# First eight and last seven dense units on all 128 rows of TensorE, with both weight halves of a unit in one tile

## The chip, the core and the metric

The kernel runs on one core of a Trainium2 chip. The metric is the device time of one execution in microseconds (us); the kernel before takes 827.67 us, the median of 3 runs (827.59 to 827.92). TensorE is called PE here, its weight loads PEld, VectorE DVE, ScalarE ACT, GpSimd POOL; SP issues most DMAs.

## The reference

Input `x` has 2048 tokens of 512 features. It is normalized, and two branches read the result: attention in a window of 256 tokens (32 heads of 16 features), and a SwiGLU block with 1792 hidden features. The block's output is a gate on the attention's output:

```python
xn = _layernorm(x)
qkv = xn @ wqkv                                  # 512 x 1536
scores = q @ k.T * 16 ** -0.5                    # masked: 0 <= i - j < 256
s = (softmax(scores) @ v) @ wo                   # 512 x 512
b = (silu(xn @ w_gate) * (xn @ w_up)) @ w_down   # 512 x 1792, 1792 x 512
return x + s * silu(b)
```

All of it is float32. Dense products are made of three matmuls: each operand is split into a rounded high part and the low part that is left, and high x high, high x low and low x high are added (`PAIRS`).

## The kernel before

**Units.** The tokens come in four chunks of 512. Dense work is cut into units, each with its own weights: `Proj` (q and k of two head groups, tiles named `a`), `GateUp` (one block of 128 hidden features, `g` and `u`), `Values` and `WideValues` (v, `vp`), `Down` (a part of w_down, `d`), `Wo` and `WideWo` (`s`). Most units have 1024 weight columns (24 steps of 512 columns), the wide ones, `WideValues`, `WideWo` and the longer `Down`, 2048. A name such as `d1_3_0` is chunk 1, part 3, item 0.

**Two lanes.** PE's 128 rows are used as two halves of 64 rows that work side by side. Lane 0 (rows 0 to 63) multiplies the first 64 features of each block of 128, lane 1 (rows 64 to 127) the other 64. Both add into the same PSUM bank, so lane 1 starts an item when lane 0 has ended it (`hand_over`, L1818; `LAG` matmuls are added to be sure). Lane 1 is thus always about one item behind lane 0. Score matmuls (`b` at L1465 for the row maxima, `c` at L1593 for the probabilities) have 48 or 49 rows and fill both lanes in pairs. Visits (`pv`, L1641) multiply probabilities with v in 64x32 pieces.

**Weights.** A raw unit of weights comes by DMA (`wr`). ACT rounds it into the high tile (`wh`, L642), POOL subtracts to get the low tile (`wl`, L647), both in halves of 512 columns. Since lane 1 lags, tile j holds the lower 64 rows of unit j and the upper 64 rows of unit j-1, and lane 1 reads tile `n + 1`. There are `NWH = 14` such tiles, so seven pairs of a high and a low half; a half is given back when both lanes have read it (`used`, L675).

**The order.** Everything is written out by a planner in Python that runs when the kernel is built. It keeps a clock for every engine, takes the unit that is due, and puts score pairs and visits at the places that the tables `EARLY`, `VIS` and `MWU` give. What it writes is the fixed order of instructions on each engine; at run time only semaphores hold an engine back.

**The two ends.** At the start `load_first` (L403) brings `x` and the first weights. `Values` for the first chunk begins as soon as the lower 64 rows of its weights are there, with lane 0 alone, and the transposes of the scaled chunk 0 that follow (`xt_turn`, L702) are made in 64x64 pieces, eight per block of 128 features. At the end the last `Wo` (L1119) evens the lanes out: lane 0 takes 22 of lane 1's 256-column matmuls, for which four DMAs (`rest_low`, L1290) copy upper rows of the attention's output to the lower rows.

Of the kernel before, what the change touches and what calls it, by code (L numbers as in the profile page):

```python
# [17 lines left out]
P = 128  # L18
R = 64
# [40 lines left out]
LAG = 7  # L60
# [18 lines left out]
MOVED = 10  # L79
# [4 lines left out]
OUT = 3.4  # L84
# [11 lines left out]
)  # L96
VIS = (
# [8 lines left out]
def tile_window_attention_swiglu_gate(  # L106
# [296 lines left out]
    def load_first():  # L403
# [66 lines left out]
        def split(raw, j, r, t):  # L470
# [5 lines left out]
            def low(a):  # L476
                hi, lo = (w[half(r)] for w in wtile[j, a // 512][:2])
                nc.gpsimd.tensor_tensor(lo, raw[half(r), a : a + 512], f32(hi), op=ALU.subtract)
                if r == 0 and a:
                    timer(free_at["G"] + SURE, raw_give, raw)  # L480

            def ready(t):
                if (j, r) == (1, 0):
                    low1.append(t)
                else:
                    wready[j, 0] = wready[j, 1] = t
# [28 lines left out]
        split(wr[0], 0, 0, (6.6, 6.85))  # L515
        split(wr[1], 1, 1, (9.35, 10.3))
        split(wr[1], 1, 0, (11.9, 11.9))
# [32 lines left out]
    def half(r):  # L550
        return slice(R * r, R * r + R)
# [5 lines left out]
    class Unit:  # L557
# [3 lines left out]
        def w(self, r, s, a, k):  # L561
            t = wtile[self.n + r, a][s]
            return t.rearrange("p (k n) -> p k n", n=self.cols)[half(r), k, :]

        def wat(self, r, a):
            return wready.get((self.n + r, a))
# [34 lines left out]
    def w_fetch(j):  # L601
        lo, up = weighted.get(j), weighted.get(j - 1)
        if lo is None and up is None:
            return
        parts = [(r, u) for r, u in ((0, lo), (1, up)) if u is not None]
        if lo is None:
            parts.append((0, up))
        box = []

        def go(r, u, last):  # L610
            if not box:
                box.append(raw_take(f"wr{j}"))
            if r == 0 and lo is None:
                move(box[0][half(0)], u[half(1)])
            else:
                move(box[0][half(r), : u.shape[1]], u[half(r)])
            if last and j:
                w_fetch(j + 1)

        for n, (r, u) in enumerate(parts):  # L620
            last = n == len(parts) - 1
            dma(now[0], lambda r=r, u=u, last=last: go(r, u, last),
                lambda t, last=last: w_split(j, t, box[0]) if last else None,
                slack=WSL, can=lambda: box or rfree)

    def w_split(j, t, raw):
        w = [weighted[i].shape[1] if i in weighted else 0 for i in (j, j - 1)]
        both = min(w)
        cuts = [(slice(0, P), a, min(a + 512, both)) for a in range(0, both, 512)]
        if max(w) > both:  # L630
            r = 0 if w[0] > both else 1
            cuts += [(half(r), both, max(w))]
        if j not in weighted:
            cuts = [(slice(0, P), a, a + 512) for a in (0, 512)]
        left = [sum(b <= 512 for _, _, b in cuts), sum(b > 512 for _, _, b in cuts), len(cuts)]

        def high(pr, a, b):
            h = a // 512
            if (j, h) not in wtile:
                w_take(j, h)  # L640
                split_next[0] = (j, 1) if h == 0 and max(w) > 512 else (j + 1, 0)
# [15 lines left out]
        def before(margin, n):  # L657
            at = work_at.get(j, total)
            return lambda: now[0] + max(at - work[0], 0.0) * PRESS - margin + 0.3 * n

        spare = now[0] + max(work_at.get(j, total) - work[0], 0.0) - t - 5.0
# [40 lines left out]
    def xt_turn(c, k):  # L702
        left = [2]
        for r in range(2):
            pb, tag = bank(rb_free, f"xp{c}_{k}_{r}")
            src = pb[:, :256].rearrange("p (t n) -> p t n", n=R)
            hi, lo = (
                xn[c % 2][s][:, k, :].rearrange("p (t r n) -> p t r n", r=2, n=R)[:, :, r, :]
                for s in range(2)
            )  # L710

            def go(t, r=r, pb=pb):
                nc.tensor.matmul(  # L713
                    pb[:, R * t : R * t + R], xt[c, t][half(r), k * P : (k + 1) * P],
                    ident[half(r), half(r)], is_transpose=True, start=True, stop=True,
                )

            def done(t, tag=tag):
                rb_free[tag] = t
                left[0] -= 1  # L720
                if left[0] == 0:
                    xready[c, k] = t
                    if k == KC - 1:
                        for i in range(4):
                            give(xt.pop((c, i)))

            def low(src=src, hi=hi, lo=lo):
                nc.vector.tensor_tensor(lo, src, f32(hi), op=ALU.subtract)

            def finished(t, src=src, hi=hi, low=low, done=done):  # L730
                do("S", t, 0.3, lambda: nc.scalar.activation(hi, src, AF.Copy),
                   lambda t: do("V", t, 0.35, low, done, 0.3), 0.3)

            for t in range(4):
                extra[r].append((128, lambda t=t, go=go: go(t), finished if t == 3 else None))
# [211 lines left out]
    class Wide(Unit):  # L947
# [3 lines left out]
        def w(self, r, s, k):  # L951
            return wtile[self.n + r + k // 2, k % 2][s][half(r)]
# [9 lines left out]
        def gate(self, i, r, m):  # L962
            k = m // 3
            return wready.get((self.n + r + k // 2, k % 2))
# [8 lines left out]
    class Values(Moving):  # L973
# [25 lines left out]
        def gate(self, i, r, m):  # L999
            kp, a, b = (m // 8, 0, m // 4 % 2) if m < 16 else ((m - 16) // 4, 1, 0)  # L1000
            return latest([(lready if a else cready).get((i, kp)), wpart.get((self.n + r, r, b, 512 * kp), 0.0 if self.n + r > 1 else None)])
# [117 lines left out]
    class Wo(Moving):  # L1119
# [15 lines left out]
        def mms(self, i, r, pb):  # L1135
# [3 lines left out]
            todo = [(t, k, PAIRS, None) for t in range(2 - r) for k in range(KC)]  # L1139
            other = [(1, k, p) for k in range(KC) for p in PAIRS]  # L1140
            cut = len(other) if i else MOVED
            todo += [(t, k, [p], xn[1]) for t, k, p in other[:cut]] if r == 0 else [(t, k, [p], None) for t, k, p in other[cut:]]
            for n, (t, k, pairs, moved) in enumerate(todo):
                po = (pb, self.second[i])[t][:, :256]
                tok = slice((2 * i + t) * P, (2 * i + t + 1) * P)
                for a, b in pairs:
                    def go(first, last, n=n, k=k, a=a, b=b, t=t, tok=tok, po=po, moved=moved, pairs=pairs):
                        end = (a, b) == pairs[-1] and [o[0] for o in todo[n + 1 :][:1]] != [t]
                        if moved:
                            act, wt = moved[a][half(0), k, i * P : i * P + P], self.n + 1  # L1150
                        else:
                            act, wt = self.act(k, a)[half(r), tok], self.n + r
                        wt = wtile[wt, k // 2][b].rearrange("p (k n) -> p k n", n=256)[half(r), k % 2, :]
                        mm(po, act, wt, r == 0 and moved is None and (k, a, b) == (0, 0, 0), end)
                        if end and (i, r, t) == (1, 0, 0):
                            hand_over(pos[0], clock[0], 0.0)
                        elif end and i + r:
                            last_part(i, t, po, now[0] + 0.35)
                    yield 256, go, k // 2

        def gate(self, i, r, m):
            if (self.c, self.hf) != (NCH - 1, 1):
                return super().gate(i, r, m)
            if m < 6:
                return 0.0
            if r or m < 6 * KC:
                return self.wat(r, 1)
            return latest([rest.get("t") if rest.get("n") == 4 else None, self.wat(1, 0), self.wat(1, 1)])
# [119 lines left out]
    rest = {}  # L1288

    def rest_low():  # L1290
        for n in range(4):
            def copy(s=n % 2, i=n // 2):
                n = i * 2 * P + P
                move(xn[1][s][half(0), :, i * P : i * P + P], xn[0][s][half(1), :, n : n + P])

            def landed(t):
                rest["n"] = rest.get("n", 0) + 1
# [709 lines left out]
```

## Time and profile before

| what | value |
|---|---|
| median of 3 runs | 827.67 us |
| the profiled execution | 827.96 us |
| its span, first to last instruction | 826.1 us |
| PE busy | 820.2 us (99%), 9874 matmuls |
| POOL / DVE / ACT busy | 640.2 / 503.7 / 497.8 us |
| PE clock granted | 1.00 |
| first dense matmul starts, last one starts | 9.12 us, 822.23 us |

A share of PE counts time in which at least one lane works, so a lane that idles beside the other isn't seen in it. A matmul's own duration is longer than the distance to the next one on its lane, since they are pipelined; what counts is the distance from start to start. One record is about 1.9 us longer than the span because of what lies around the program's first and last instruction.

### The profile page before, as it was taken

How to read it: one execution, taken by the hardware profiler on the slowest of the kernel's cores; microseconds unless marked ns; L12 is line 12 of the kernel's file. 1: busy time of each engine (PE TensorE's matmuls, PEld its weight loads, DVE VectorE, ACT ScalarE, POOL GpSimd, SP SyncE). 2: the span in 40 equal slices, each digit the busy share in tenths (PEclk: the TensorE clock that was granted, in tenths of full speed). 3: DMA queues.
4: the chain of work that ended last, by engine and by line, in shares of the span. 5: the costliest groups of instructions: out<-in, count | busy, mean ns of one | idle time of the engine just before them, and what ended most of it. 6: DMA issues, size and time to landing. Idle time of an engine off the chain costs nothing.

```text
span 826.1 us, 25672 instructions
## 1 busy us (share of the span) xinstructions
PE 820.2 (99%) x9874; PEld 702.4 (85%) x9874; DVE 503.7 (61%) x1545; ACT 497.8 (60%) x949; POOL 640.2 (77%) x898
## 2 busy tenths in 40 slices
PE   8999999999999999999999999999999999999998
PEld 8999888888888888888889888888888888888887
DVE  4246688456657786656648786557546556644235
ACT  6536866465666667456766757546667664566532
POOL 6566878887768799669877789858688976896963
PEclk9999999999999999999999999999999999999999
DMA  6596766686678785577668876566786787864344
GB/s 168 153 214 172 176 155 171 166 192 162 155 198 215 207 226 123 134 204 172 167 151 206 204 197 182 145 168 148 189 189 155 165 175 205 198 134 109 80 124 129
DMA packets 67810, 140.13 MB, mean 170 GB/s; under 512 B 14742, under 2 KB 18326, under 8 KB 67688
## 3 DMA queue, kind: packets, MB, share of 16 engines
q1 hardware_dynamic: 67224, 137.84, 67.7%
q8 instruction: 78, 1.28, 0.7%
q10 hardware_dynamic: 464, 0.66, 0.3%
q14 instruction: 44, 0.36, 0.2%
HBM read 107.74 MB, written 29.62 MB: 166 GB/s over the span
## 4 chain that ended last, share of the span: by engine, by line
PE 99%; DMA 1%; DVE 0%; SPq 0%; issue 0%; DVEq 0%
PE d L693 20%; PE u L693 19%; PE g L693 18%; PE a L693 10%; PE pv L1641 9%; PE c L1593 6%; PE vp L693 6%; PE s L693 6%; PE b L1465 5%; DMA xt<-x 1%; PE xp L525 0%; PE xp L713 0%; DVE st L422 0%; SPq L147 0%; DVE xt L427 0%; PE warm L309 0%
## 5 line engine op out<-in xcount | busy, mean ns | idle before, releaser
L647 POOL TENSOR_TENSOR wl<-wr,wh 128x512 fp32r<-128x512 f32 x238 | 305.8, 1299 | 65.8 <-ACT wh L642 55.2
L1473 DVE CUSTOM_DVE_ANT_0 jk<-b,maskb 128x384 bf16<-128x384 f32 (+2 forms) x512 | 250.2, 528 | 104.8 <-PE b L1465 91.4
L1553 ACT ACTIVATE p<-c 128x512 f32<-128x512 f32 (+2 forms) x384 | 197.9, 569 | 67.0 <-PE c L1593 61.1
L693 PE MATMUL d<-wh,hh 64*128 64x512 f32 x896 | 221.1, 390 | 0.0
L693 PE MATMUL u<-xl,wh 64*128 64x512 f32 x448 | 162.5, 390 | 0.0
L693 PE MATMUL g<-xh,wh 64*128 64x512 f32 x448 | 162.5, 389 | 0.0
L693 PE MATMUL u<-xh,wh 64*128 64x512 f32 x448 | 162.4, 389 | 0.0
L693 PE MATMUL g<-xh,wl 64*128 64x512 f32 x448 | 161.6, 389 | 0.0
L693 PE MATMUL u<-xh,wl 64*128 64x512 f32 x448 | 161.4, 389 | 0.0
L693 PE MATMUL g<-xl,wh 64*128 64x512 f32 x448 | 160.6, 389 | 0.0
L642 ACT ACTIVATE wh<-wr 128x512 fp32r<-128x512 f32 x238 | 144.5, 630 | 24.9 <-PE d L693 17.0
L693 PE MATMUL d<-wl,hh 64*128 64x512 f32 x448 | 158.8, 390 | 0.0
L693 PEld LDWEIGHTS d<-wh,hh 64*128 64x128 f32 x896 | 141.2, 185 | 13.4 <-issue 0.4
L1565 POOL TENSOR_SCALAR_AFFINE_SELECT p<-p 128x256 f32<-128x256 f32 x256 | 101.6, 410 | 40.0 <-ACT p L1553 38.7
L1569 POOL TENSOR_SCALAR_AFFINE_SELECT p<-p 128x256 f32<-128x256 f32 x224 | 91.3, 411 | 9.9 <-ACT p L1553 9.6
L887 POOL TENSOR_TENSOR hh<-h,hh 128x512 fp32r<-128x512 f32 x53 | 68.8, 1298 | 36.4 <-ACT hh L883 34.5
L693 PE MATMUL a<-xh,wh 64*128 64x512 f32 x256 | 96.2, 389 | 0.0
L693 PE MATMUL a<-xl,wh 64*128 64x512 f32 x256 | 95.8, 388 | 0.0
L693 PE MATMUL a<-xh,wl 64*128 64x512 f32 x256 | 95.7, 387 | 0.0
L1465 PE MATMUL b<-k,q 48*128 48x384 f32 (+2 forms) x512 | 90.6, 326 | 0.0
L1593 PE MATMUL c<-q,k 49*128 49x128 f32 (+2 forms) x704 | 89.0, 298 | 0.0
L693 PEld LDWEIGHTS d<-wl,hh 64*128 64x128 f32 x448 | 82.5, 185 | 6.5 <-issue 0.2
(130 smaller groups left out, 1943.2 us busy)
## 6 DMA issues: line engine op xcount, KB each, us to landing
wr<-wgu SPq DMA_DIRECT2D x112, 256.0 KB
wr<-wdn SPq DMA_DIRECT2D x48, 256.0 KB
k<-qkd SPq DMA_DIRECT2D x48, 192.0 KB
wr<-wqk SPq DMA_DIRECT2D x32, 256.0 KB
q<-qkd SPq DMA_DIRECT2D x64, 128.0 KB
od<-ev SPq DMA_DIRECT2D x32, 256.0 KB
qkd<-qkh SPq DMA_DIRECT2D x31, 256.0 KB
qkd<-qkl SPq DMA_DIRECT2D x29, 256.0 KB
```

The costliest lines, as they stand in the source:

```text
L642: nc.scalar.activation(wtile[j, h][0][pr, a - 512 * h : b - 512 * h], raw[pr, a:b], AF.Copy)
L647: nc.gpsimd.tensor_tensor(lo, raw[pr, a:b], f32(hi), op=ALU.subtract)
L693: recent[0] = nc.tensor.matmul(pb, a, b, start=first, stop=last, skip_group_check=True).ins
L887: nc.gpsimd.tensor_tensor(hl[:, 1, :], self.h, f32(hl[:, 0, :]), op=ALU.subtract)
L1465: nc.tensor.matmul(pb[:, :n], qs[u % 3][r : r + 48, p, qb * P : (qb + 1) * P], ks[u % 3][r : r + 48, p, lo : lo + n], start=True, stop=True,)
L1473: nc.vector.tensor_tensor_reduce(junk[:, :n], pb[:, :n], maskb[:, 3 * P - n :], 1.0, -3.0e38, ALU.add, ALU.max, m[:, col : col + 1],)
L1553: nc.scalar.activation(t[:, h, :], pc[:, :n], AF.Exp, scale=DH ** -0.5)
L1565: nc.gpsimd.affine_select(s, s, [[0, 2], [1, P]], ALU.is_ge, 0.0, base=0, channel_multiplier=-1)
L1569: nc.gpsimd.affine_select(s, s, [[0, 2], [-1, P]], ALU.is_gt, 0.0, base=0, channel_multiplier=1)
L1593: nc.tensor.matmul(pc[:, at0 : at0 + w], ks[u % 3][r : r + 49, p, k0 : k0 + P], qs[u % 3][r : r + 49, p, qb * P : qb * P + w], start=(i == ...
L1641: nc.tensor.matmul(pbs[r][0][32 * j : 32 * j + 32, q0:q1], vt[half(r), (4 * c + kb) % VT, VW * (4 * g + j) : VW * (4 * g + j) + 32], t[hal ...
```

## The change

The planner gets a second way to issue dense work. For the first eight units (`NFULL`) and the last seven (`TAIL`) it issues one matmul over all 128 rows where it issued a pair of 64-row matmuls; the units between stay in two lanes. These are 300 matmuls of 512 columns and 192 of 256 columns in the place of as many pairs. Before it changes from one way to the other, the lane that is ahead waits until both have ended the same unit. Both 64-row halves of a unit's weights now lie in one tile (`wtile[self.n]`), so the first DMAs of weights bring 128 rows each. The transposes of chunk 0 are whole 128x128 ones, the evening out at the end with its four DMAs is gone, `LAG` goes from 7 to 3, and the tables that place scores and visits have new numbers. One `WideWo` (chunk 1) comes one unit earlier.

```diff
-LAG = 7
+LAG = 3
-MOVED = 10
+NFULL = 8
+TAIL = 7
+WSH = 0
-OUT = 3.4
+OUT = 3.009
...
-    -0.179, -0.21, -0.095, -0.4, -0.388, 0.119, 0.067, -0.001,
+    -0.106, -0.21, -0.038, -0.4, -0.388, 0.119, 0.067, -0.15,
...
         for a, eng in ((512, nc.scalar), (0, nc.sync)):
-            move(wr[0][half(0), a : a + 512], u0[half(0), a : a + 512], eng)
+            move(wr[0][:, a : a + 512], u0[:, a : a + 512], eng)
         rows(2, nc.scalar)
         rows(3, nc.sync)
         for a in (0, 512):
-            move(wr[1][half(1), a : a + 512], u0[half(1), a : a + 512])
-        move(wr[1][half(0)], u1[half(0)])
+            move(wr[1][:, a : a + 512], u1[:, a : a + 512])
...
         def w(self, r, s, a, k):
-            t = wtile[self.n + r, a][s]
+            t = wtile[self.n, a][s]
...
     def used(r, n, a, t):
-        half_ended.add((r, n, a))
-        j = n + r
-        if all((h, j - h, a) in half_ended or j - h not in weighted or weighted[j - h].shape[1] <= 512 * a for h in range(2)):
-            timer(t, w_end, j, a)
+        for h in range(2) if r == 2 else (r,):
+            half_ended.add((h, n, a))
+        if all((h, n, a) in half_ended for h in range(2)):
+            timer(t, w_end, n, a)
...
+    def both_rows(n):
+        return stream[n][0].n < NFULL or stream[n][0].n >= order[-TAIL].n
+
+    def full():
+        return pos[0] == pos[1] < len(stream) and both_rows(pos[0]) and not any(extra)
...
+    def full_mm():
+        n = pos[0]
+        u, i = stream[n]
...
+        go(m == 0, m == len(todo) - 1)
...
+        pos[:] = [n + 1] * 2
...
         if r == 0:
+            if pos[1] < pos[0] and both_rows(pos[0]):
+                return None
```

Where the first eight units end, PE's order before goes on in two lanes; `wh8_0` is the first high half of tile 8, `g0_4` the first unit behind the eight:

```order
L1465 MATMUL b0_2_0_962<-k0_77,q0_74 128x384
L1465 MATMUL b0_2_1_963<-k0_77,q0_74 128x384
L693 MATMUL g0_4_968<-xh0_81,wh8_0_790 128x512
L693 MATMUL g0_3_877<-xh0_81,wl8_0_791 128x512
L693 MATMUL g0_4_968<-xl0_82,wh8_0_790 128x512
```

At the same place of PE's order now:

```order
L678 MATMUL g0_4_695<-xl0_82,wh8_0_595 128x512
L678 MATMUL g0_4_695<-xh0_81,wl8_0_596 128x512
L678 MATMUL g0_4_695<-xh0_81,wh8_0_595 128x512
L678 MATMUL g0_4_695<-xl0_82,wh8_0_595 128x512
L678 MATMUL g0_4_695<-xh0_81,wl8_0_596 128x512
L678 MATMUL u0_4_738<-xh0_81,wh8_1_603 128x512
```

Before, `g0_4` on lane 0 alternates with `g0_3` on lane 1; now all twelve matmuls of `g0_4` and four of `u0_4` stand on lane 0 before lane 1's first dense matmul, with score pairs among them.

Where chunk 2's `WideValues` (`vp2`) meets chunk 1's last `Down` (`d1_3`), both wide, PE's order before, with `d1_3_0` on lane 0 and `vp2` on lane 1:

```order
L693 MATMUL d1_3_0_7948<-wh63_0_7836,hh1_12_7211 128x512
L693 MATMUL vp2_3_7875<-wh61_0_7486,xh0_81 128x512
L693 MATMUL d1_3_0_7948<-wh63_1_7897,hh1_13_7388 128x512
L693 MATMUL vp2_3_7875<-wl61_0_7487,xh0_81 128x512
L693 MATMUL d1_3_0_7948<-wl63_1_7898,hh1_13_7388 128x512
```

The same units on PE now:

```order
L678 MATMUL d1_3_0_7645<-wh63_0_7489,hh1_12_6910 128x512
L678 MATMUL vp2_3_7576<-wl60_1_7141,xh0_81 128x512
L678 MATMUL vp2_3_7576<-wh60_1_7140,xl0_82 128x512
L678 MATMUL vp2_3_7576<-wh61_0_7196,xh0_81 128x512
L678 MATMUL vp2_3_7576<-wl61_0_7197,xh0_81 128x512
L678 MATMUL vp2_3_7576<-wh61_0_7196,xl0_82 128x512
L678 MATMUL vp2_3_7576<-wh61_1_7274,xh0_81 128x512
L678 MATMUL vp2_3_7576<-wl61_1_7275,xh0_81 128x512
L678 MATMUL vp2_3_7576<-wh61_1_7274,xl0_82 128x512
L678 MATMUL d1_3_0_7645<-wh63_1_7682,hh1_13_7055 128x512
```

Lane 1 now ends `vp2` with seven matmuls that have no partner, and only then comes the half tile `wh63_1`, which lies at the address of `wh60_0` and is written when lane 1 has read that one for the last time; the next eight dense matmuls stand on lane 0 alone.

Where the last seven units begin, PE's order before, in two lanes through `g3_10` and `g3_11`:

```order
L693 MATMUL g3_11_14356<-xh1_83,wh111_0_14089 128x512
L693 MATMUL g3_10_14249<-xl1_84,wh111_0_14089 128x512
L693 MATMUL g3_11_14356<-xl1_84,wh111_0_14089 128x512
L693 MATMUL g3_10_14249<-xh1_83,wl111_0_14090 128x512
L693 MATMUL g3_11_14356<-xh1_83,wl111_0_14090 128x512
```

At the same place now (the last rows of lane 1, then the first ones over 128 rows):

```order
L678 MATMUL u3_10_13975<-xh1_83,wh110_1_13796 128x512
L678 MATMUL u3_10_13975<-xl1_84,wh110_1_13796 128x512
L678 MATMUL u3_10_13975<-xh1_83,wl110_1_13797 128x512
L678 MATMUL g3_11_14064<-xh1_83,wh111_0_13805 128x512
L678 MATMUL g3_11_14064<-xl1_84,wh111_0_13805 128x512
L678 MATMUL g3_11_14064<-xh1_83,wl111_0_13806 128x512
```

Lane 0 has ended `u3_10` when lane 1 still has five matmuls of `g3_10` and all twelve of `u3_10` to do, and `g3_11` doesn't start before they are done.

More of the change, by code (lines that the diff above doesn't have):

```diff
@@ L478, in low @@
                 nc.gpsimd.tensor_tensor(lo, raw[half(r), a : a + 512], f32(hi), op=ALU.subtract)
-                if r == 0 and a:
+                if a:
                     timer(free_at["G"] + SURE, raw_give, raw)
             def ready(t):
-                if (j, r) == (1, 0):
+                if j:
                     low1.append(t)
-                else:
-                    wready[j, 0] = wready[j, 1] = t
+                wready[j, 0] = wready[j, 1] = t
             for a in (0, 512):
@@ L514, in load_first @@
             do("V", lands[i], 1.05 if i != 1 else 1.45, lambda i=i: stats(i), lambda t, i=i: after_stats(t, i), -1.0)
-        split(wr[0], 0, 0, (6.6, 6.85))
-        split(wr[1], 1, 1, (9.35, 10.3))
-        split(wr[1], 1, 0, (11.9, 11.9))
+        split(wr[0], 0, 2, (6.9, 7.9))
+        split(wr[1], 1, 2, (11.0, 11.9))
     def x_turn(i):
@@ L550, in half @@
     def half(r):
-        return slice(R * r, R * r + R)
+        return slice(0, P) if r == 2 else slice(R * r, R * r + R)
     def latest(times):
@@ L561, in w @@
         def w(self, r, s, a, k):
-            t = wtile[self.n + r, a][s]
+            t = wtile[self.n, a][s]
             return t.rearrange("p (k n) -> p k n", n=self.cols)[half(r), k, :]
         def wat(self, r, a):
-            return wready.get((self.n + r, a))
+            return wready.get((self.n, a))
         def inputs(self, i):
@@ L601, in w_fetch, with go @@
     def w_fetch(j):
-        lo, up = weighted.get(j), weighted.get(j - 1)
-        if lo is None and up is None:
+        u = weighted.get(j)
+        if u is None:
             return
-        parts = [(r, u) for r, u in ((0, lo), (1, up)) if u is not None]
-        if lo is None:
-            parts.append((0, up))
         box = []
-        def go(r, u, last):
+        def go(r):
             if not box:
                 box.append(raw_take(f"wr{j}"))
[L613 to L617, printed above, removed]
+            move(box[0][half(r), : u.shape[1]], u[half(r)])
+            if r:
                 w_fetch(j + 1)
[L620 to L623, printed above, removed]
+        for r in range(2):
+            dma(now[0], lambda r=r: go(r), lambda t, r=r: w_split(j, t, box[0]) if r else None,
                 slack=WSL, can=lambda: box or rfree)
     def w_split(j, t, raw):
[L627 to L634, printed above, removed]
+        w = weighted[j].shape[1]
+        cuts = [(slice(0, P), a, a + 512) for a in range(0, w, 512)]
         left = [sum(b <= 512 for _, _, b in cuts), sum(b > 512 for _, _, b in cuts), len(cuts)]
@@ L640, in high @@
                 w_take(j, h)
-                split_next[0] = (j, 1) if h == 0 and max(w) > 512 else (j + 1, 0)
+                split_next[0] = (j, 1) if h == 0 and w > 512 else (j + 1, 0)
             nc.scalar.activation(wtile[j, h][0][pr, a - 512 * h : b - 512 * h], raw[pr, a:b], AF.Copy)
@@ L657, in before @@
         def before(margin, n):
-            at = work_at.get(j, total)
+            at = work_at.get(j + WSH, total)
             return lambda: now[0] + max(at - work[0], 0.0) * PRESS - margin + 0.3 * n
-        spare = now[0] + max(work_at.get(j, total) - work[0], 0.0) - t - 5.0
+        spare = now[0] + max(work_at.get(j + WSH, total) - work[0], 0.0) - t - 5.0
         t += min(max(0.5 * spare, 0.0), 1.5)
@@ L702, in xt_turn, with done, low @@
     def xt_turn(c, k):
[L703 to L709, printed above, removed]
-            )
[L712 to L735, printed above, removed]
+        pb, tag = bank(rb_free, f"xp{c}_{k}")
+        hi, lo = (xn[c % 2][s][:, k, :] for s in range(2))
+        for t in range(4):
+            nc.tensor.matmul(
+                pb[:, P * t : P * t + P], xt[c, t][:, k * P : (k + 1) * P], ident,
+                is_transpose=True, start=True, stop=True,
+            )
+        advance(0.45)
+        def done(t):
+            rb_free[tag] = t
+            xready[c, k] = t
+            if k == KC - 1:
+                for i in range(4):
+                    give(xt.pop((c, i)))
+        def low():
+            nc.vector.tensor_tensor(lo, pb, f32(hi), op=ALU.subtract)
+        do("S", now[0] + 0.2, 0.52, lambda: nc.scalar.activation(hi, pb, AF.Copy),
+           lambda t: do("V", t, 0.61, low, done, 0.3), 0.3)
     def x_wait(c):
@@ L951, in w @@
         def w(self, r, s, k):
-            return wtile[self.n + r + k // 2, k % 2][s][half(r)]
+            return wtile[self.n + k // 2, k % 2][s][half(r)]
         def wneed(self, i, r):
@@ L963, in gate @@
             k = m // 3
-            return wready.get((self.n + r + k // 2, k % 2))
+            return wready.get((self.n + k // 2, k % 2))
         def mms(self, i, r, pb):
@@ L1000, in gate @@
             kp, a, b = (m // 8, 0, m // 4 % 2) if m < 16 else ((m - 16) // 4, 1, 0)
[L1001 removed]
+            return latest([(lready if a else cready).get((i, kp)), wpart.get((self.n, r, b, 512 * kp))])
         def inputs(self, i):
@@ L1138, in mms, with go @@
                 return
[L1139 to L1143, printed above, removed]
+            for t in range(2):
                 po = (pb, self.second[i])[t][:, :256]
                 tok = slice((2 * i + t) * P, (2 * i + t + 1) * P)
[L1146 to L1159, printed above, removed]
+                for k in range(KC):
+                    for a, b in PAIRS:
+                        def go(first, last, k=k, a=a, b=b, t=t, tok=tok, po=po):
+                            end = (k, a, b) == (KC - 1, *PAIRS[-1])
+                            mm(po, self.act(k, a)[:, tok], self.w(r, b, k // 2, k % 2), (k, a, b) == (0, 0, 0), end)
+                            if end:
+                                last_part(i, t, po, now[0] + 0.35)
+                        yield 256, go, k // 2
         def gate(self, i, r, m):
@@ L1163, in gate @@
                 return super().gate(i, r, m)
[L1164 to L1168, printed above, removed]
+            return 0.0 if m % 12 < 6 else self.wat(r, 1)
         def begin(self, i):
@@ L1286, in gates @@
         return all(gready.get((NCH - 1, t), 1e9) <= now[0] for t in ts)
[L1288 to L1297, printed above, removed]
-                rest["t"] = t
-            dma(now[0], copy, landed, 0.0, 128, lambda: NCH - 1 in x_used)
     def x_landed(i):
@@ L1402, in split @@
             oready[c, k] = t
-            if last and all((c, n) in oready for n in range(KC)):
-                timer(t, rest_low)
         def then_r(t):
@@ L1860, in next_mm, with full_ready @@
             u.done(i, banks.pop(n), t, lambda t: fb_free.__setitem__(tag, t))
+    def both_rows(n):
+        return stream[n][0].n < NFULL or stream[n][0].n >= order[-TAIL].n
+    def full():
+        return pos[0] == pos[1] < len(stream) and both_rows(pos[0]) and not any(extra)
+    def full_ready():
+        u, i = stream[pos[0]]
+        if run[0] is not None:
+            return u.gate(i, 2, run[0][1])
+        return latest([bank_time(fb_free), u.inputs(i), u.wneed(i, 2)])
+    def full_mm():
+        n = pos[0]
+        u, i = stream[n]
+        if run[0] is None:
+            banks[n], tags[n] = bank(fb_free, u.name(i))
+            if isinstance(u, Wo):
+                u.begin(i)
+            run[0] = [list(u.mms(i, 2, banks[n])), 0]
+        todo, m = run[0]
+        cols, go, a = todo[m]
+        go(m == 0, m == len(todo) - 1)
+        advance(max(cols * 0.000417, 0.1067) + 0.0025)
+        work[0] += cols * MM / 512
+        if u.last_use(i) and all(o[2] != a for o in todo[m + 1 :]):
+            n2, a = a if isinstance(u, Wide) else (0, a)
+            used(2, u.n + n2, a, clock[0] + 0.2)
+        run[0][1] += 1
+        if run[0][1] < len(todo):
+            return
+        run[0] = None
+        pos[:] = [n + 1] * 2
+        tag = tags.pop(n)
+        u.done(i, banks.pop(n), clock[0] + 0.2, lambda t: fb_free.__setitem__(tag, t))
     def ready(r):
@@ L1911, in tile_window_attention_swiglu_gate @@
             continue
-        times = [ready(0), ready(1)]
+        whole = full()
+        times = [full_ready()] * 2 if whole else [ready(0), ready(1)]
         able = [r for r in range(2) if times[r] is not None and times[r] <= max(clock[r], now[0])]
@@ L1955, in tile_window_attention_swiglu_gate @@
             idle = 0
+            if whole:
+                full_mm()
+                continue
             r = min(able, key=lambda r: clock[r])
```

22 rows, old and new, of tables (EARLY, MWU, VIS) are left out of this document.

## The prediction

> **What bounds the kernel now.** I read the page first, then the chain, PE's waits, the windows by stage, and the timeline of PE at both ends.
>
> ```profile
> PE 820.2 (99%) x9874; PEld 702.4 (85%) x9874; DVE 503.7 (61%) x1545; ACT 497.8 (60%) x949; POOL 640.2 (77%) x898
> PE 99%; DMA 1%; DVE 0%; SPq 0%; issue 0%; DVEq 0%
> PE warm L309 <- DVE warm L304: 1.1, 1, 1.1
> PE xp L525 <- issue: 0.7, 1, 0.7
> PE xp L525 <- DVE xt L427: 0.5, 1, 0.5
> 56.00:770.00 714.00, 714.00 (x8713) 604.38 (x8712) 462.83 (x1466) 447.37 (x856) 570.10 (x828) 1.00 0.71 174
> 822.30:826.10 3.80, 0.20 (x2) 0.00 (x0) 0.93 (x3) 0.00 (x0) 0.75 (x2) 1.00 0.40 138
> ```
>
> PE is the chain (99%). Its waits sum to 2.3 us, all before 9.1 us, and between 56 and 770 us it is busy for 714.00 of 714.00 us. So nothing that another engine does faster can gain there: the time is the sum of the distances between matmuls, plus about 9 us ahead of the first and 3.6 us behind the last. A change gains by shorter distances or by filling a lane that stands empty while the other works, and loses wherever PE is made to wait. The distances, in the timeline of PE:
>
> ```profile
> 788.22 0.39 PE L693 MATMUL g<-xh,wh 64*128 64x512 f32 x1
> 788.45 0.39 PE L693 MATMUL u<-xh,wh 64*128 64x512 f32 x1
> 788.45 0.39 PE L693 MATMUL g<-xl,wh 64*128 64x512 f32 x1
> ...
> 788.90 0.39 PE L693 MATMUL u<-xh,wl 64*128 64x512 f32 x1
> 788.90 0.39 PE L693 MATMUL g<-xh,wh 64*128 64x512 f32 x1
> 821.63 0.28 PE L693 MATMUL s<-wh,xh 64*128 64x256 f32 x1
> ...
> 822.23 0.28 PE L693 MATMUL s<-wh,xl 64*128 64x256 f32 x1
> 6.33 0.27 PE L525 MATMUL xp<-ident,xt 128*128 128x128 f32 x1
> 6.44 0.83 PE L309 MATMUL warm<-warm 128*128 128x128 f32 x6
> ```
>
> Three pairs of 512 columns go from 788.22 to 788.90: 0.227 us a pair. Six lone matmuls of 256 columns start at even distances from 821.63 to 822.23: 0.120 us, the same with or without a partner. Matmuls over all 128 rows exist in one form alone, 128x128 in true f32. They come 0.11 us apart: from 6.33 to 6.44, and (0.83 - 0.275)/5 = 0.111 for the six (0.275 us being one's duration).
>
> **The change part by part.**
>
> *Distances (gain).* No row shows a rounded 128-row matmul of 256 or 512 columns. The nearest is the f32 transpose, about 0.110. From 256 to 512 columns a lane's distance grows by 0.227 - 0.120 = 0.107, which I read as the streaming of 256 columns; the rest is 0.013 in a lane and 0.003 over 128 rows, so a transpose streams as long as 256 columns do, and I take its distance for them. That makes 0.110 and 0.217 for 256 and 512 columns, 0.010 less than a lane each. Over a longer stretch of the chain pairs are a little dearer:
>
> ```profile
> 793.82 14.64 PE d L693 x128
> ```
>
> 64 pairs in 14.64 us are 0.2288 each, by which 512 columns save 0.012. I take 0.011 for 300 + 192 = 492 matmuls: 5.4 us. Bounds: 3.4 us (0.113, what rounding leaves open for the six warm-up matmuls, saves 0.007) and 6.4 us (streaming alone, 0.013).
>
> *Empty lane at the start and the evening out (gain).*
>
> ```profile
> 9.12 0.74 PE L693 MATMUL vp<-wh,xh 64*128 64x256 f32 x4
> 11.43 0.63 PE L693 MATMUL vp<-wl,xh 64*128 64x256 f32 x4
> 11.99 0.66 PE L525 MATMUL xp<-ident,xt 128*128 128x128 f32 x4
> 12.57 0.62 PE L693 MATMUL vp<-wh,xl 64*128 64x256 f32 x3
> 15.06 0.28 PE L693 MATMUL vp<-wl,xh 64*128 64x256 f32 x1
> 15.17 0.28 PE L693 MATMUL vp<-wh,xh 64*128 64x256 f32 x1
> ```
>
> From 9.12 to about 15 one lane works alone. The last `Wo` pays it back by giving 22 of lane 1's matmuls to lane 0, so lane 0 carries 44 more than lane 1: 44 x 0.120 = 5.3 us in which lane 1 is empty, worth half of that, 2.65 us of span. All of it goes.
>
> *Changes of tile shape (gain).* The four matmuls at 11.43 are (0.63 - 0.28)/3 = 0.117 apart, so the last starts at 11.78; the transpose follows 0.21 later, 0.09 more than a plain distance. The order has 69 such changes before and 66 now: 0.25 us.
>
> *Two new passages (cost).* Where eight units end, sixteen matmuls of 512 columns stand on lane 0 alone (twelve of `g0_4`, four of `u0_4`), less what lane 1's score matmuls overlap: 15 x 0.227/2 = 1.7 us. Where the last seven begin, seventeen stand on lane 1 alone: 17 x 0.227/2 = 1.9 us. Bounds: none to speak of, the order fixes them.
>
> *Two wide units in a row (cost).* At `vp2` and `d1_3` seven matmuls on lane 1 and then eight on lane 0 have no partner; the ends of each overlap a little, 13 x 0.227/2 = 1.5 us. The new wait is that of lane 0 for `wl63_1`:
>
> ```profile
> L647 POOL TENSOR_TENSOR wl<-wr,wh 128x512 fp32r<-128x512 f32 x238 | 305.8, 1299 | 65.8 <-ACT wh L642 55.2
> L642 ACT ACTIVATE wh<-wr 128x512 fp32r<-128x512 f32 x238 | 144.5, 630 | 24.9 <-PE d L693 17.0
> ```
>
> After lane 1's last read of `60_0`, ACT (0.63) and POOL (1.30) must write the half: 1.93 us and some 0.6 us of matmul end and semaphores (0.39 is the matmul's own duration), against eleven distances, 2.5 us, until it is read. PE waits for 0 to 0.5 us; all of PE's queue stands behind it, the score pairs of visit 18 first, for which DVE waits. With 0.1 us: 1.6 us.
>
> *Transposes (cost).* In the chain from 10 to 24 us the 64-row ones hold 7.0%:
>
> ```profile
> by line: PE vp L693 83.2%; PE xp L525 8.4%; PE xp L713 7.0%; PE a L693 1.7%
> ```
>
> Of 14 us that is 1.0; sixteen whole ones at 0.11 are 1.75. Cost 0.8 us.
>
> *Loads at the start (cost).* The first weights are now 128 rows each, 256 KB more ahead of `x`'s last two blocks. The window up to 9.1 us, and ACT centering these two blocks:
>
> ```profile
> 0.00:9.10 9.10, 6.80 (x42) 6.26 (x42) 3.65 (x11) 3.99 (x7) 4.74 (x16) 1.00 0.71 189
> 9.44 0.72 ACT L430 ACTIVATE xt<-xt,nm 128x512 f32<-128x512 f32 x1
> 10.84 0.72 ACT L430 ACTIVATE xt<-xt,nm 128x512 f32<-128x512 f32 x1
> ```
>
> At 189 GB/s (the last number) they land 1.4 us later. But ACT centers the last block at 10.84 at the earliest, behind `xh` copies and roundings, and in the new order one rounding fewer stands ahead of it; I take its transposes as coming at the same 12 us. Up to their end PE now has twelve full matmuls and eight transposes to do, 20 x 0.11 = 2.2 of the 3.5 us from 9.12 (a wait of 1.3), where lane 0 had 16 x 0.12 + 8 x 0.11 + 4 x 0.09 = 3.2 (a wait of 0.3). Of these 1.0 us some is won back behind, where the weights of the second unit are early for the later PE. Cost 0.6 us, between 0.2 and 1.4.
>
> *One answer each.* Fewer, larger evictions of the transposes, the four DMAs of the end and the moved `WideWo` lie beside a PE that is never idle: nothing. `LAG` and the tables shift the places; the distances don't depend on the place. The chain from the last visit to `Wo`'s second operand has 115 x 0.2165 = 24.9 us of dense work to hide it, where 29.5 hid it; by the order's POOL and ACT rows and the 1.30 and 0.63 above it ends with the half tile freed by `d3_3_3`, about when `Wo`'s eighteenth matmul needs it: 0 to 0.5 us, taken as 0.
>
> *Sum.* Gains 5.4 + 2.65 + 0.25 = 8.3; costs 1.7 + 1.9 + 1.6 + 0.8 + 0.6 = 6.6; net gain 1.7 us. The profiled execution would take 827.96 - 1.7 = 826.3 us; it lies 0.29 above the median of 827.67, so the forecast for the median is 826.0 us.
>
> **The rivals.** *Waits take the gain, no change.* The 128-row distance is nearer to 0.113 (2.0 us less), or PE waits for late half tiles here and there. For it: POOL is 77% busy and feeds every unit. Against it: the order before has every score pair placed by the same rules, and PE's waits show none behind 9.1 us. With 0.5 to 2.5 us less gain: 826.5 to 828.5, typically 827.2. About 0.2%, 1.7 us, is what a measurement of this kernel can tell from no change; the forecast lies on that line, so cases a little short of it count here too.
>
> *Slower: half tiles run out.* A half is now held until both lanes have ended with it, and two wide units need eight where seven exist. If `vp2` and `d1_3` aren't the only such place, each costs 1.6 us; eighteen wide units lie in the two-lane stretch. One more place takes the gain, from the third on (3 x 1.6 - 1.7 = 3.1) it is slower by over 0.2%: 830.8 us. Against it: at that place alone does the order leave a lane without dense work.
>
> *Slower: weights not loaded ahead.*
>
> ```profile
> L525 PEld LDWEIGHTS xp<-ident,xt 128*128 128x128 f32 x16 | 1.7, 140 | 1.8 <-issue 0.9 <-DVE xt L427 0.7
> L693 PEld LDWEIGHTS d<-wh,hh 64*128 64x128 f32 x896 | 141.2, 185 | 13.4 <-issue 0.4
> ```
>
> A lane's load could hide only beside the other lane's matmul. Full matmuls would then stand behind their own loads, 492 x 0.185 = 91 us more: 917 us. The rows speak against it: transposes with loads of 0.140 us come 0.11 apart, and lane 0 alone runs at 0.12 with loads of 0.185. The Trainium skill has this rule ("TensorE: Matmul & The Clock Gate", Part 3: a weight load overlaps with matmuls in flight only when the row group differs); by that rule the change would be a heavy loss, and the trace disagrees with it.
>
> *The change does nothing:* excluded, the order shows the full matmuls.
>
> **How the numbers follow.** The sum holds, a gain of 1.2 to 3.3 us: 0.60, with four fifths of it over the line. Waits or the wider distance: 0.33. Half tiles run out: 0.05. Loads not hidden: 0.02. The sum's cases over the line and a few of better places give faster 0.52, the rest of them and the second case same 0.41, the last two and the worst waits slower 0.07. Range: the better bounds of the distances (1.0 more), of the start (0.4) and of `wl63_1` (0.1) give 824.5, rounded out to 824.4; the narrower distances (2.0 less) alone give 828.0, which with 827.9 as the upper end leaves the slower cases out and about a tenth.
>
> **What would show it.** Right: full matmuls 0.216 and 0.109 apart; PE's waits grow by about a microsecond before 13 us and by under half at `d1_3_0`; one lane alone for some 3.6 us where the eighth unit ends and again before `g3_11`; the last matmul near 820.5. Wrong: distances of 0.22 and more; PE waiting for `wl` or `wh` between 56 and 770 us; a wait ahead of `Wo`.

## The result and the profile after

The changed kernel takes 835.46 us in the median (834.12 to 837.71, four runs) against 827.63 us before (827.19 to 827.92): ratio 1.0098, 95% interval 1.0075 to 1.0121. A repetition (e5 below) gave 834.99, ratio 1.0091 (1.0077 to 1.0105). The forecast was 826.0, faster or the same; it became slower by 7.8 us. The four runs now spread over 3.6 us, where they spread over 0.7. The profiled execution of the changed kernel is the longest of its four, 837.71 us with a span of 836.0 (before: 827.96 and 826.1), so the trace shows more than the typical loss; e5's profile (835.63, span 833.9) lies nearer to the median.

The page after: busy time of the engines, then the shares of the chain that ended last.

```profile
PE 826.6 (99%) x9366; PEld 703.6 (84%) x9366; DVE 501.9 (60%) x1541; ACT 486.5 (58%) x933; POOL 625.4 (75%) x886
PE 90%; DMA 6%; DVE 2%; ACT 1%; issue 0%; SPq 0%; ACTq 0%; POOL 0%; DVEq 0%; POOLq 0%
```

PE issues 508 matmuls fewer (9366 for 9874) and is busy 6.4 us longer: fewer, but not shorter. A tenth of the chain now leaves PE (a twentieth in e5's profile), where 1% did. PE's waits (us in total, times, longest), and the same stretch of the middle as before (us, PE busy, the other engines, clock):

```profile
PE b L1408 <- DMA k<-qkd: 2.1, 1, 2.1
PE vp L678 <- ACT xh L544: 1.3, 1, 1.3
PE warm L311 <- DVE warm L306: 1.1, 1, 1.1
PE xp L524 <- ACT xt L432: 0.4, 1, 0.4
PE b L1408 <- DVE h L842: 0.3, 1, 0.3
PE c L1536 <- DMA q<-ms: 0.2, 1, 0.2
PE pv L1584 <- DVE m L1416: 0.2, 1, 0.2
56.00:770.00 714.00, 711.14 (x8622) 603.92 (x8622) 461.00 (x1463) 432.47 (x837) 554.69 (x807) 1.00 0.73 173
```

The middle, where PE was busy for 714.00 of 714.00 us, now has 2.9 us in which it is not. No wait is for a weight half (`wl`, `wh`): all are for scores and visits, a bank, or the start (the warm-up and `x`). The full matmuls in PE's timeline, 512 columns and the last ones of 256:

```profile
30.08 0.39 PE L678 MATMUL a<-xh,wh 128*128 128x512 f32 x1
...
30.76 0.39 PE L678 MATMUL g<-xh,wh 128*128 128x512 f32 x1
...
831.91 0.28 PE L678 MATMUL s<-wl,xh 128*128 128x256 f32 x1
832.03 0.28 PE L678 MATMUL s<-wh,xl 128*128 128x256 f32 x1
```

0.227 us apart for 512 columns (0.68 for three, from 30.08 to 30.76) and 0.120 for 256: what a pair of lanes took. The gain of 5.4 us is not there, and distances of 0.22 and more were the first sign of being wrong that the prediction named.

Where the time goes is read by finding the same unit's first matmul of lane 0 in the timelines (counted off along the program's order) and taking the difference:

| first matmul of | before | after | e5 | later: after, e5 |
|---|---|---|---|---|
| `vp0_0_0` (the first dense one) | 9.12 | 10.06 | 8.76 | 0.9, -0.4 |
| `a0_0` | 23.39 | 25.30 | 24.68 | 1.9, 1.3 |
| `s0_0` | 274.86 | 279.39 | 276.24 | 4.5, 1.4 |
| `g3_0` | 629.55 | 637.31 | 635.12 | 7.8, 5.6 |
| `g3_10` | 763.90 | 772.16 | 770.02 | 8.3, 6.1 |
| `g3_11` | 770.19 | 782.45 | 780.34 | 12.3, 10.2 |
| `s3_1_0` (last Wo) | 813.83 | 826.39 | 824.27 | 12.6, 10.4 |
| the last matmul | 822.23 | 832.03 | 829.91 | 9.8, 7.7 |

Four places stand out. The start loses 1.3 to 1.9 us (in e5 the first `vp` is early, but PE then waits 1.2 us ahead of the transposes of `x`); the chain from the program's start goes through the later blocks of `x`:

```profile
2.93 7.12 DMA xt<-x
...
10.07 0.70 DVE st L424
...
12.23 0.73 ACT xt L432
...
13.00 0.66 PE xp L524 x4
```

At the first score pair of unit 8, before `s0_0`, PE stands from 207.34 until `k` has landed:

```profile
207.01 0.33 PE L1408 MATMUL b<-k,q 48*128 48x384 f32 x1
209.48 0.58 PE L1408 MATMUL b<-k,q 48*128 48x384 f32 x3 [2.13 <-DMA k<-qkd]
```

In this execution SP issued that `k` late. Its last two transfers in SP's timeline, after and then before, there with the first pair in PE's timeline:

```profile
202.16 0.96 SPq L149 DMA_DIRECT2D k<-qkd  x2
```

```profile
193.57 0.89 SPq L147 DMA_DIRECT2D k<-qkd  x2
202.96 0.51 PE L1465 MATMUL b<-k,q 48*128 48x384 f32 x4
```

5 us ahead of the pair here, 9 us before. e5 shows below that this is not the kernel's order but this execution's.

The third place lies between `s0_0` and `g3_0` and holds `vp2`/`d1_3` and two more waits; it is taken up below. The fourth is the exit passage: lane 1 alone, until `g3_11` starts over 128 rows.

```profile
778.72 0.39 PE L678 MATMUL g<-xh,wl 64*128 64x512 f32 x1
778.95 0.39 PE L678 MATMUL g<-xh,wh 64*128 64x512 f32 x1
...
782.13 0.39 PE L678 MATMUL u<-xh,wl 64*128 64x512 f32 x1
782.45 0.50 PE L678 MATMUL g<-xh,wh 128*128 128x512 f32 x1
```

Lane 0 waits 17 distances there, 4.0 us by the table. At the end 2.8 us come back (12.6 to 9.8), since lane 0 no longer does 22 matmuls of lane 1.

### The profile page after: what moved, and what is told of

Same layout as the page of the kernel before. It is cut to its first block, busy times and chain, and to the rows that moved or that the text cites. A ratio compares the mean times of both kernels' runs of the same rounds, so it can differ in the third digit from the quotient of the medians.

```text
span 836.0 us, 24658 instructions
## 1 busy us (share of the span) xinstructions
PE 826.6 (99%) x9366; PEld 703.6 (84%) x9366; DVE 501.9 (60%) x1541; ACT 486.5 (58%) x933; POOL 625.4 (75%) x886
## 4 chain that ended last, share of the span: by engine, by line
PE 90%; DMA 6%; DVE 2%; ACT 1%; issue 0%; SPq 0%; ACTq 0%; POOL 0%; DVEq 0%; POOLq 0%
PE u L678 18%; PE d L678 18%; PE g L678 16%; PE a L678 10%; PE pv L1584 8%; PE c L1536 6%; PE vp L678 5%; PE s L678 5%; PE b L1408 4%; DMA qkd<-qkl 2%; DMA q<-ms 1%; DMA q<-qkd 1%; DMA xt<-x 1%; DMA k<-qkd 1%; DMA qkd<-wide 1%
## 5 line engine op out<-in xcount | busy, mean ns | idle before, releaser
L678 PE MATMUL d<-wh,hh 64*128 64x512 f32 (+1 forms) x840 | 207.3, 390 | 0.0
L678 PE MATMUL u<-xh,wl 64*128 64x512 f32 (+1 forms) x420 | 160.4, 390 | 0.0
L678 PE MATMUL u<-xh,wh 64*128 64x512 f32 (+1 forms) x420 | 160.3, 390 | 0.0
L678 PE MATMUL g<-xh,wh 64*128 64x512 f32 (+1 forms) x420 | 160.3, 389 | 0.0
L678 PE MATMUL u<-xl,wh 64*128 64x512 f32 (+1 forms) x420 | 160.0, 390 | 0.0
L678 PE MATMUL g<-xh,wl 64*128 64x512 f32 (+1 forms) x420 | 159.9, 390 | 0.0
L678 PE MATMUL g<-xl,wh 64*128 64x512 f32 (+1 forms) x420 | 159.7, 389 | 0.0
L678 PE MATMUL d<-wl,hh 64*128 64x512 f32 (+1 forms) x420 | 146.2, 391 | 0.1
L678 PEld LDWEIGHTS d<-wh,hh 64*128 64x128 f32 (+1 forms) x840 | 133.9, 185 | 14.1 <-issue 0.6
L678 PE MATMUL a<-xl,wh 64*128 64x512 f32 (+1 forms) x240 | 86.8, 389 | 0.0
```

The costliest lines, as they stand in the source:

```text
L678: recent[0] = nc.tensor.matmul(pb, a, b, start=first, stop=last, skip_group_check=True).ins
```

## The experiments

The theory after the result: (1) rounded full matmuls are as far apart as lanes, since the 0.013 us over the streaming belongs to the type and not to the rows; (2) the losses forecast (start, passages, `vp2`/`d1_3`) are real and now stand alone; (3) the rest is waits at score places. The rivals: the shorter distance depends on the load or the accumulation and could still be had; the planner's too short price of a full matmul brings the waits; the tables do.

**e1, the distance by itself.** Groups of 16 matmuls behind the last one of the changed kernel.

```
+    groups = [
+        ("ma", 16, lambda i: (w0, w1)[i % 2][:, :P], lambda i: mv, 0),
+        ("mb", 16, lambda i: (w0, w1)[i % 2][:, :P], lambda i: mv[:, :256], 0),
...
+        ("me", 16, lambda i: w0[:, :P], lambda i: mv, 0),
+        ("mf", 16, lambda i: (w0, w1)[i % 2][:, :P], lambda i: mv, 1),
...
+        ("mj", 16, lambda i: idb[:, :P], lambda i: mkb[:, :512], 0),
+        ("mk", 16, lambda i: idb[:, :P], lambda i: mkb[:, :256], 0),
```

> The changed kernel with twelve groups of matmuls appended behind its last one; their sums are used by nothing. In the changed kernel the 128-row matmul of rounded f32 comes every 0.227 us (512 columns) and 0.120 (256), as a 64-row lane does, while the true f32 transpose over 128 rows comes every 0.11, that is 0.003 over the 0.107 that 256 columns stream. Theory A, the 0.013 belongs to the rounded form, whatever the rows: rounded groups 0.227 (512), 0.173 (384), 0.120 (256), the lone lane 0.227 and a pair of lanes 0.227, the same weights each time 0.227, a new sum each time 0.227; bf16 of 512 and 256 columns 0.217 and 0.110. Theory B, it belongs to the exchange of weights (two different tiles in turn): the group with the same weights 0.217, bf16 with its own load as the rounded one. Theory C, it belongs to adding into a bank that holds a sum: the group with a new sum each time 0.217. Theory D, every matmul of one pass has it and only the transposes are without: bf16 0.227 and 0.120 too. 128 columns in 0.067 would show that loads of 0.188 us never hold a matmul up; about 0.188 or more that they do.

The timeline of PE at the end of e1 (a row with xN holds N matmuls from the first one's start to the last one's end):

```profile
833.12 0.28 PE L1973 MATMUL mbb<-xh,xh 128*128 128x256 f32 x1
833.24 0.28 PE L1973 MATMUL mbb<-xh,xl 128*128 128x256 f32 x1
...
839.55 3.87 PE L1973 MATMUL mea<-xh,xh 128*128 128x512 f32 x16
...
846.43 0.39 PE L1973 MATMUL mfb<-xh,xh 128*128 128x512 f32 x1
846.66 0.39 PE L1973 MATMUL mfb<-xh,xl 128*128 128x512 f32 x1
...
860.42 1.91 PE L1973 MATMUL mka<-maskb,ident 128*128 128x256 bf16 x16
862.16 3.60 PE L1973 MATMUL mlb<-xh,xh 128*128 128x512 f32 x8
```

Rounded: 0.120 (256), 0.174 (384), 0.227 (512, a new sum each time), 0.228 (adding on), 0.232 with the same weights each time, (3.87 - 0.39)/15; that mean holds the long first distance of its group, whose last eight are 0.227 apart. bf16: (1.91 - 0.27)/15 = 0.109 for 256 and, from single starts, 0.2155 for 512. True f32 of 512 columns (the last row) leaves two records a matmul, (3.60 - 0.59)/7 = 0.430 apart, close to the 0.428 that four times 0.107 make. Theory A: neither another tile of weights nor a new sum matters, the type does. What in the type costs the 0.013 stays open, since no group is without loads: a rounded matmul has one of 0.188 us, with the same weights too, a bf16 one has one of 0.097. Rounded matmuls of 128 columns came 0.111 apart, neither the 0.067 nor the 0.188 expected. The Trainium skill ("TensorE: Matmul & The Clock Gate", Part 1) gives N / 2.4 GHz + 2.5 ns for a warm matmul, 215.7 ns at 512; the bf16 groups agree, the rounded ones are 11 ns longer.

**e2, both ends in lanes again.**

```
-NFULL = 8
-TAIL = 7
+NFULL = 0
+TAIL = 1
...
-... wpart.get((self.n, r, b, 512 * kp)) ...
+... wpart.get((self.n, 2, b, 512 * kp)) ...
```

> The changed kernel with the first eight and last six units in two lanes again; the last unit stays full, weights, tables and loads stay as changed. Theory A, full matmuls are as far apart as pairs of lanes: the two passages go (15 and 17 distances of 0.227 in which one lane is alone, half of it, 3.6 us), and lane 1 is empty again at the start (31 distances of 0.120) and lane 0 at the end (31 of 0.120 and 5 of 0.227), half of 8.6, 4.3 us: 0.7 us slower than the changed kernel's 835.5, 835 to 837. Theory B, full matmuls save the 5.4 us forecast and something else took more: 840 to 842. Theory C, planning the full stretch with a distance too short (0.216 for 0.227) is what brings the waits of the middle: these go with it, 3 us of 4, and the time is 832 to 834.

835.04 us, ratio to before 1.0100 (1.0084 to 1.0115): 0.4 below the changed kernel's first median, 0.05 above its second. B is out: the full matmuls' distances are worth nothing. C is out too, since the loss stays without a full stretch. A holds, at its lower edge.

**e3, one unit between the two wide ones.**

```
+            elif order and isinstance(order[-1], WideValues) and isinstance(ffn[0], Down):
+                u = ffn.pop(1)
```

> The changed kernel with d1_3 put one GateUp unit later, so that vp2 and d1_3 no longer follow each other; the order of PE is the same up to vp2. Theory: two wide units in a row hold more half tiles than there are; the place cost 2.3 us in the profiled execution (8 matmuls alone on each lane, half of 16 x 0.227, 1.8, and a wait of 0.5 to 0.9): 833 to 834.2, and no stretch with one lane alone there. Rival: the lanes only shift, what is lost there is lost at the next wide unit: 835 to 836.

833.46 us (832.46 to 833.84), ratio 1.0071 (1.0059 to 1.0084): 1.5 to 2.0 less than the changed kernel. The place cost what the forecast said, 1.6.

**e4, the planner's price of a full matmul.**

```
-        advance(max(cols * 0.000417, 0.1067) + 0.0025)
+        advance(cols * 0.000417 + 0.0133)
```

> The changed kernel with the planner's price of a full matmul set to the measured distance (0.0133 us over the streaming instead of 0.0025, 0.227 for 0.216). The order of PE stays the same but for a few score pairs. Theory A, the plan of the full stretch runs 2.6 us ahead of the chip (240 matmuls x 0.0108), transfers are issued against that plan, and this brings PE's waits for k, q and ms between 200 and 470 us: they go, 832 to 833.5. Theory B, the waits come from the order of the transfers on SP (weights ahead of q and k loads, SP standing behind transfers under way), which the price hardly touches: 834.5 to 836.5, and PE still waits for k or q for over 1.5 us in the sum.

835.07 us, ratio 1.0092 (1.0078 to 1.0106). The time is B's, and A is out. By the span (first to last instruction) e4's median is 0.65 us below that of e5, the changed kernel run again: its times are 2.4 us longer than the spans, e5's 1.7, and nothing here explains why. The 2 us and more of theory A are not there either way. But B's second half missed: in e4's profile PE waits for no `k` and no `q`. That wait is not the kernel's as such; e5 asks whether it comes and goes.

**e5, the changed kernel again.**

> The changed kernel itself, nothing altered. In e3 and e4, whose code and whose order of PE are the same up to 40 us and more, the first vp started at 8.8 and 9.0 us instead of 10.06, and PE did not wait 2.1 us for k at the first pair of unit 8. Theory A, these two losses belong to the one profiled execution (when x lands, how SP's transfers fall): 834 to 835.5, first vp near 9, no such wait. Theory B, they belong to the kernel and the edits of e3 and e4 took them away: 835.5 to 837.7 with both in the profile.

834.99 us (834.17 to 835.63). PE's waits in its profile:

```profile
PE warm L311 <- DVE warm L306: 1.1, 1, 1.1
PE c L1536 <- DMA q<-ms: 1.1, 1, 1.1
PE xp L524 <- ACT xt L432: 0.9, 2, 0.6
PE b L1408 <- DVE h L842: 0.3, 1, 0.3
PE xp L524 <- DVE xt L429: 0.3, 1, 0.3
PE pv L1584 <- DVE m L1416: 0.2, 1, 0.2
```

A: no wait for `k`, the first `vp` at 8.76. The last `k` in SP's timeline, and the pair in PE's:

```profile
196.52 1.76 SPq L149 DMA_DIRECT2D k<-qkd  x2
206.36 0.55 PE L1408 MATMUL b<-k,q 48*128 48x384 f32 x4
```

That is 9.8 us ahead, by the same order of instructions. Instead there is a wait for `q<-ms` that was 0.2 in the other execution; SP issued that transfer 8.9 us before PE was ready for it, and in the kernel before 8.1 us sufficed. Which transfer is late differs from one execution to the next, and one wait stays: the third score pair of unit 11.

```profile
278.03 0.46 PE L1408 MATMUL b<-k,q 48*128 48x384 f32 x2
278.20 0.39 PE L678 MATMUL s<-wl,xh 64*128 64x512 f32 x1
...
279.36 0.33 PE L1408 MATMUL b<-k,q 48*128 48x384 f32 x1
279.95 0.44 PE L1408 MATMUL b<-k,q 48*128 48x384 f32 x1 [0.26 <-DVE h L842]
280.43 0.50 PE L678 MATMUL s<-wh,xh 64*128 64x512 f32 x1
```

From the pair to the next dense matmul 1.07 us pass, where the pair ahead of it needed 0.17. The wait list shows 0.3 of these 0.9 us: it counts from the end of the earlier matmul.

**e6, the old tables on the new layout.** `EARLY`, `VIS` and `MWU`, `LAG = 7` and `OUT = 3.4` as before.

> The changed kernel with the tables EARLY, VIS and MWU, LAG and OUT of the kernel before. Theory A, the new tables fit the score and visit places to half tiles that are now held until both lanes have ended: with the old ones lanes stand alone at more places (by the order 25 more distances with one lane alone, half of 25 x 0.227, 2.8 us, and shorter stretches): 838 to 841. Theory B, the new tables are what brings the waits of score pairs (0.9 us at the third pair of unit 11 in every profile so far): 832 to 834.

836.81 us, ratio 1.0116 (1.0102 to 1.0130): 1.8 slower than e5, less than A gave. Its profile shows no wait at all behind the start:

```profile
PE warm L311 <- DVE warm L306: 1.1, 1, 1.1
PE vp L678 <- ACT xh L544: 1.0, 1, 1.0
PE vp L678 <- POOL wl L480: 0.2, 1, 0.2
```

So both theories may hold a part: the old tables bring no wait, and cost time all the same. That it goes into lanes that stand alone for longer, as the order says, was not measured, and whether the new tables or the new `LAG` and `OUT` bring the waits isn't shown, since all three changed together.

**e7, another way to the shorter distance.** On the kernel before, as e1's bf16 groups suggest.

```
+    def top(ap):
+        return ap.bitcast(BF16)[:, 1::2]
+
-    def mm(pb, a, b, first, last):
+    def mm(pb, a, b, first, last, cross=0):
+        if cross:
+            a, b = top(a), top(b)
```

> The kernel before, not the changed one, with the two cross products of every dense product (high by low and low by high) fed as bf16: the upper 16 bits of the same rounded tiles, read at a stride of two, without any added instruction. The lower 16 bits of both operands are left out of the cross products. e1 measured 0.2155 and 0.109 us between bf16 matmuls of 512 and 256 columns, 0.2267 and 0.1195 between rounded ones. Theory A, the overhead of 0.011 goes with the type, in lanes too: two thirds of some 2,780 pairs save 0.0112 each, 20.8 us: 806 to 809 if no other engine falls behind, up to 815 with waits of PE for scores and half tiles. Theory B, bf16 at a stride of two streams as four-byte data does, or exchanging types costs what it saves: 826 to 829.

840.48 us, ratio 1.0157 (1.0143 to 1.0171), with PE still never waiting behind 9 us. Both theories missed. One lane's triples (high by high in rounded f32, then the two cross products in bf16) in the timeline:

```profile
795.39 0.59 PE L698 MATMUL g<-xh,wh 64*128 64x512 f32 x1
...
796.10 0.59 PE L698 MATMUL g<-xh,wh 64*128 64x512 f32 x1
...
796.80 0.59 PE L698 MATMUL g<-xh,wh 64*128 64x512 f32 x1
```

0.705 us a triple, where three rounded pairs take 0.680.

**e8, why.** Groups of rounded (f), strided bf16 (t) and plain bf16 (c) matmuls behind the changed kernel, as in e1.

> The changed kernel with fourteen groups of matmuls of 512 columns appended, whose sums are used by nothing: rounded f32 (f), bf16 read as the upper halves of the same tiles at a stride of two (t), and bf16 read without a stride (c), over 128 rows and as pairs of lanes, alone and mixed. In e7 a triple f, t, t took some 0.70 us a pair of lanes instead of the 0.68 of three f and the 0.66 that 0.2267 + 2 x 0.2155 would make. Theory A, the stride costs: t alone 0.23 or more, c 0.2155, and mixed groups no dearer than their parts. Theory B, the exchange of types costs: t alone 0.2155 over 128 rows and in lanes, f and t in turn 0.24 each, and four f with eight t in blocks less than 0.2267 on the mean. Theory C, lanes of bf16 don't overlap as lanes of rounded f32 do: t over 128 rows 0.2155, in pairs of lanes 0.23 or more.

Over 128 rows: a strided moving operand (mb, mc), and a plain one with strided weights (md).

```profile
836.00 0.39 PE L1986 MATMUL mbb<-xh,xl 128*128 128x512 bf16 x1
836.23 0.39 PE L1986 MATMUL mbb<-xh,xh 128*128 128x512 bf16 x1
836.68 3.77 PE L1986 MATMUL mca<-xh,ident 128*128 128x512 bf16 x16
840.29 0.38 PE L1986 MATMUL mdb<-maskb,xh 128*128 128x512 bf16 x1
840.50 0.38 PE L1986 MATMUL mdb<-maskb,xl 128*128 128x512 bf16 x1
```

mc: (3.77 - 0.39)/15 = 0.225; md 0.2155. The stride of the moving operand costs 0.010, in lanes too (0.225 a pair, plain 0.2157). f and t in turn take 0.233 over 128 rows and 0.236 a pair in lanes (both from the second start of the group to the last), where the mean of f and t is 0.226. A triple f, t, t in lanes takes 0.701, near e7's 0.705; its parts would make 0.677. A and B each hold a part, C falls. So e7 saved next to nothing on each bf16 matmul (0.002) and paid for every change of type.

**e9 and e10, mending what is left.** Both with e3's edit and `LAG = 1` for 3; e10 also with

```
-MARG = 0.046
+MARG = 0.2
```

> e3 (d1_3 one unit later) with LAG 1 instead of 3, so that lane 1 follows lane 0 two matmuls earlier: by the order 15 instead of 17 matmuls of lane 1 stand alone where the last seven units begin. Theory A: lane 0's wait there is what the exit passage costs, 2 x 0.227 = 0.45 us go, and nothing else moves: 832.6 to 833.4. Theory B, lane 1 now reaches a bank before lane 0's last matmul in it has ended and PE waits at every unit: 834 or more.

> e9 with MARG 0.2 instead of 0.046: the planner lets a score pair wait 0.15 us longer for its bank before it places it. In the changed kernel the third score pair of unit 11 has stood up PE for 0.9 us in every profile, since DVE reads the bank's former tile later than planned. Theory A: the plan of the banks is too tight for this order; with the margin that wait goes and the time is 0.9 lower than e9's, 831.7 to 832.5. Theory B: the margin only moves the pairs and other places wait (for q or ms on SP's queue): within 0.5 of e9.

e9: 832.11 us (831.28 to 832.68), ratio 1.0054 (1.0041 to 1.0068), 1.35 below e3, more than the 0.45 of the exit and below the range of either theory: its list has no wait behind the start, where e3's had 0.7 for `q<-ms` and 0.3 for a bank. e10: 831.47 (831.18 to 834.0), ratio 1.0053 (1.0040 to 1.0065). The median is 0.64 below e9's, between what the two theories gave, and within e9's spread, so the runs don't decide; at unit 11 the dense matmul comes 0.40 behind the pair in both, so the margin shows nothing there. The best form of the change that I found is still 4 us above the kernel before.

## Why the prediction was wrong, by its own steps

*Distances (gain of 5.4): this is the step that failed.* It read 0.013 "in a lane and 0.003 over 128 rows" and took the transposes' distance "for them". The transposes are true f32, the dense matmuls rounded; I gave to the rows what belongs to the type. Nor could a row of 128 columns give the distance of 256: rounded matmuls over 128 rows come 0.111 apart at 128 columns, as the transposes do, and 0.120 at 256 (e1). The rounded lane, alone or paired, was the nearer row, and it stood quoted beside the other; even the lower bound (3.4) left it out. Measured: 0, by the rows above, e1 and e2. With this term at 0 the sum is a loss of 3.7 us.

*Loads and transposes at the start (1.4):* right in size, 1.3 to 1.9 at `a0_0`, and it changes by execution.

*Passages and evening out (1.7 + 1.9 - 2.65 - 0.25 = 0.7):* right in kind. In e5's column of the table they are 0.1 around the entry, 4.1 at the exit, 0.2 behind it, less 2.7 at the end: 1.7. Lane 0 loses next to nothing at the entry and all of it at the exit.

*Two wide units in a row (1.6):* right, by e3.

*"Beside a PE that is never idle: nothing", and the tables "shift the places; the distances don't depend on the place":* the second step that failed. The distances don't, the waits do. In e5, between `s0_0` and `g3_0`, 4.2 us are lost: some 1.7 at `vp2`/`d1_3`, 0.9 at unit 11, 1.1 for `q<-ms`, and about 0.5 unaccounted for. These two waits and the unaccounted part (2.5), 0.5 up to `g3_10`, unaccounted for too, and 1.0 more at the passages make up the 4.0 us between the 3.7 of the sum without the distances and e5's 7.7.

*The rivals.* "Waits take the gain" was right to doubt the distance and to name waits, but had the wrong price, since it kept a gain of 3.4 to set against them. By the order, half tiles ran out at one place only. Weights not loaded ahead is excluded: e1's rounded matmuls over 128 rows come 0.120 apart, each with a load of its own of 0.19 (the groups of e1, busy us and mean ns of a load):

```profile
L1973 PEld LDWEIGHTS mbb<-xh,xl 128*128 128x128 f32 x8 | 1.5, 191 | 0.0
```

What stays open: why some transfers now come too late in one execution and not in the next. The lead of SP's issues alone doesn't tell: `k` had 5 us in one execution and 9.8 in the other, and `q<-ms` waited with a lead of 8.9 where 8.1 was enough before. e4 excludes the planner's price as the cause of the lost time. The profiles of e6 (old tables, `LAG` 7) and of e9 and e10 (new tables, `LAG` 1, `d1_3` moved) list no such waits, but each is one execution. That the start's loss comes from the larger first loads was read from the chain, not tried.

## What to carry to other kernels

Take a matmul's distance from a row of the same type and the same number of columns, whatever its rows; a row of the same rows and another type is the farther one. Where one engine is the bound and its order is planned tightly, a new order can bring waits of its own even if every step is costed right; leave a term for them (here about 2 us), and take a second profile of the same kernel before giving one wait a cause in the order. And going from lanes back to full matmuls waits for the lane that lags, here 17 distances or 4.1 us.

## What the runs showed of the hardware that was not expected

Rounded f32 carries 0.013 us over its streaming (0.107 for 256 columns) at 256, 384 and 512 columns, bf16 0.002. At 128 columns rounded f32 doesn't get shorter in step: 0.111, nearly the 0.120 of 256. A bf16 moving operand read at a stride of two costs 0.010 at 512 columns, a strided stationary one nothing. Changing between the types costs 0.007 a matmul over 128 rows and 0.010 to 0.012 a pair in lanes. The same kernel's transfers fell differently in two executions: one `k` was issued 5 us ahead of its use and 9.8 us.
